# Attention block on one Trainium2 core: transposing U by DMA and normalising it on GpSimd, with a dense q tile moved into the prologue

## Chip, cores, metric

One core of one Trainium2 chip. The metric is the device time of one execution in microseconds (us), median of several; the fast executions of one kernel within a set of runs spread by 0.1 to 0.6% here.

## Reference

A layer norm, multi-query attention (32 query heads of 20, one shared key and value head), and a dense feed-forward branch, all added to the input:

```python
B, S, D, H = 1, 2048, 640, 32          # head size 20
F = 1728
xn = layernorm(x)
q = (xn @ wq) as [B, H, S, 20];  k = xn @ wk;  v = xn @ wv
p = softmax(einsum("bhqd,bkd->bhqk", q, k) * 20 ** -0.5)
o = einsum("bhqk,bkd->bhqd", p, v) as [B, S, 640] @ wo
out = x + o + silu(xn @ w1) @ w2       # bf16 inputs
```

The softmax needs 32 x 2048 x 2048 exponentials, and those are the bulk of the work outside TensorE.

## The kernel before

The kernel is written as a small list scheduler. It knows estimated durations, decides for each engine the order of its instructions, and then emits them. The order is fixed when the kernel is built; the chip only waits on semaphores.

A *unit* is one head and one chunk of 512 queries (128 units). Three units make a *group* (43 groups, the last has two), and a group goes through 16 key tiles, one *step* each (688 steps). A step is three score matmuls (L735) into three PSUM banks, one ACT exponential over two or three of them (L753), and, where `want_dve` allows, VectorE's approximate exponential of the third block (L767, followed by the integer additions L825 on up to three blocks at once). The results are multiplied with V and accumulated in bank 6 (L813). What stands there at a group's end is *U*: the unnormalised outputs of its three units, with the sums by which they are to be divided.

```python
def want_dve(self, t):                       # may VectorE take the third block of step t?
    if t < DVE_FROM or t % KT >= KT - NOD:
        return False
    back = sc.t["dve"] - sc.t["pe"]          # how far VectorE is behind, by the builder's estimates
    for op in sc.pend["dve"]:
        back += op.dur
    back += len(self.zblocks) * 0.6
    return back < DVE_TH

def end_group(self, g):                      # U is in bank 6: three units and their sums
    def evac(v):
        return v.tensor_copy(self.U[0:rows, up, :], self.bk(UBANK, 0, QW, 0, rows))
    sc.new("dve", ..., evac, [("UB",)], [("U", up)], ...)
    def ut(pe):                              # transpose on TensorE, back into the same bank
        for qt in range(4):
            ins = pe.matmul(self.bk(UBANK, qt * 64, qt * 64 + 64),
                            self.U[0:rows, up, qt * P:(qt + 1) * P], self.stk[0:rows, :], ...)
    ...
    sc.new("dve", 0.14, lambda v: v.reciprocal(rl, xv[:, :, :, DH]), [("UB",)], ...)
    ...                                      # DVE: o = U transposed * reciprocal, out of the same bank
```

Beside attention, TensorE computes the q tiles of later chunks, the feed-forward branch (h: L991, its product: L1053) and the output product (L1058). `PRO` lists the projection jobs of the prologue in order (v: value tiles, t: transposes, k: key tiles, q: q tiles); the first *dense* q tile, whose rows are brought into place by seven small SBUF-to-SBUF DMA copies, was queued behind the prologue (`jobs.append(qs.pop(0))`).

The softmax here doesn't subtract the row's maximum and nothing guards it: scores larger than these inputs give would overflow.

## Time and profile before

| | before |
|---|---|
| time, median of fast runs | 772.9 us |
| span in the profile | 770.8 us |
| PE / DVE / ACT / POOL busy | 737.9 / 690.1 / 724.5 / 23.5 us |
| last exponential ends | 749.8 us |
| from there to the end | 21.0 us |

In the views PE is TensorE, PEld its weight loads, DVE VectorE, ACT ScalarE, POOL GpSimd, and SPq the queue of SyncE, which issues the DMAs. A *hole* is an idle gap of ACT, the *tail* the time from the last exponential to the end.

How to read the table: three engines are 90% busy or more, so the shares do not name the bound. What tells is who waits for whom. The prediction shows these lines. In the timelines: start us, length us, engine, line, operation, count, in brackets the idle time before it.

### The profile page before, as it was taken

How to read it: one execution, taken by the hardware profiler on the slowest of the kernel's cores; microseconds unless marked ns; L12 is line 12 of the kernel's file. 1: busy time of each engine (PE TensorE's matmuls, PEld its weight loads, DVE VectorE, ACT ScalarE, POOL GpSimd, SP SyncE). 2: the span in 40 equal slices, each digit the busy share in tenths (PEclk: the TensorE clock that was granted, in tenths of full speed). 3: DMA queues.
4: the chain of work that ended last, by engine and by line, in shares of the span. 5: the costliest groups of instructions: out<-in, count | busy, mean ns of one | idle time of the engine just before them, and what ended most of it. 6: DMA issues, size and time to landing. Idle time of an engine off the chain costs nothing. (4 is left out here: it accounts for less than half of the span.)

```text
span 770.8 us, 17543 instructions
## 1 busy us (share of the span) xinstructions
PE 737.9 (96%) x6892; PEld 241.6 (31%) x6892; DVE 690.1 (90%) x1375; ACT 724.5 (94%) x780; POOL 23.5 (3%) x68
## 2 busy tenths in 40 slices
PE   8798999999999999999999999999999999999997
PEld 4332232222233333222223333332223333222334
DVE  7976999989998998999999998899998799899985
ACT  7887999999999999999999999999999999999960
POOL 5420000000000000000000000000000000000000
PEclk9988999999999999999999999999999999999999
DMA  6650000000110000000002000000020000000100
GB/s 182 163 188 8 8 14 8 9 8 15 36 35 26 18 9 25 26 9 1 1 4 50 9 25 25 19 13 3 1 36 19 18 19 18 1 2 1 29 1 35
DMA packets 33110, 21.53 MB, mean 28 GB/s; under 512 B 20838, under 2 KB 32390, under 8 KB 33030
## 3 DMA queue, kind: packets, MB, share of 16 engines
q1 hardware_dynamic: 31718, 20.36, 9.7%
q8 instruction: 56, 0.92, 0.5%
q10 hardware_dynamic: 1312, 0.05, 0.1%
q14 instruction: 24, 0.20, 0.1%
HBM read 11.36 MB, written 2.62 MB: 18 GB/s over the span
## 5 line engine op out<-in xcount | busy, mean ns | idle before, releaser
L753 ACT ACTIVATE sbt<-psall 128x1024 bf16<-128x1024 f32 (+2 forms) x688 | 692.4, 1146 | 20.5 <-PE psall L735 18.5
L767 DVE TENSOR_SCALAR sbt<-psall 128x512 int16<-128x512 f32 x572 | 383.8, 685 | 49.7 <-PE psall L735 41.0
L735 PE MATMUL psall<-sbt 32*128 32x512 bf16 x2048 | 270.7, 387 | 18.7 <-ACT sbt L753 8.9
L813 PE MATMUL psall<-sbt 128*32 128x512 bf16 x3355 | 262.8, 387 | 0.2
L825 DVE TENSOR_SCALAR sbt<-sbt 128x1536 int16<-128x1536 int16 (+2 forms) x430 | 207.7, 505 | 4.4 <-PE psall L813 2.0
L735 PEld LDWEIGHTS psall<-sbt 32*128 32x128 bf16 x2048 | 69.4, 91 | 257.7 <-ACT sbt L753 117.9
L813 PEld LDWEIGHTS psall<-sbt 128*32 128x32 bf16 x3355 | 70.7, 95 | 114.2 <-issue 68.1
L991 PE MATMUL psall<-sbt 128*128 128x512 bf16 (+1 forms) x280 | 88.9, 390 | 2.1 <-DVE sbt L1004 1.6
L1053 PE MATMUL psall<-sbt 128*128 128x320 bf16 x448 | 87.3, 303 | 1.0 <-DVE sbt L966 0.9
L1053 PEld LDWEIGHTS psall<-sbt 128*128 128x128 bf16 x448 | 35.1, 97 | 44.5 <-issue 33.2
L1004 DVE SCALAR_TENSOR_TENSOR sbt<-sbt,psall 128x512 bf16<-128x512 bf16 (+1 forms) x56 | 38.2, 682 | 3.9 <-ACT sbt L999 3.3
L999 ACT ACTIVATE sbt<-psall 128x512 bf16<-128x512 f32 (+1 forms) x56 | 39.3, 702 | 0.0
L887 DVE CAST sbt<-psall 128x512 bf16<-128x512 f32 x43 | 29.5, 685 | 4.9 <-PE psall L813 4.8
L991 PEld LDWEIGHTS psall<-sbt 128*128 128x128 bf16 (+1 forms) x280 | 19.4, 98 | 42.7 <-issue 31.1
L1058 PE MATMUL psall<-sbt 128*128 128x320 bf16 x160 | 30.4, 302 | 0.7 <-DVE sbt L1036 0.7
L959 PE MATMUL psall<-sbt 128*128 128x512 bf16 (+1 forms) x95 | 28.6, 385 | 0.0
L672 PE MATMUL psall<-sbt 128*128 128x512 bf16 (+3 forms) x91 | 25.3, 406 | 1.7 <-POOL sbt L1201 1.4
L659 PE MATMUL psall<-sbt 128*32 128x512 bf16 (+9 forms) x74 | 21.5, 346 | 0.0
L1076 DVE SCALAR_TENSOR_TENSOR sbt<-psall,sbt 128x320 bf16<-128x320 f32 x32 | 15.0, 484 | 4.1 <-PE psall L1058 3.1
L922 DVE TENSOR_TENSOR sbt<-psall,sbt 128x240 bf16<-128x240 f32 (+2 forms) x46 | 17.2, 379 | 0.2
L1058 PEld LDWEIGHTS psall<-sbt 128*128 128x128 bf16 x160 | 12.6, 97 | 13.1 <-issue 7.0
L966 DVE TENSOR_SCALAR sbt<-psall 128x512 bf16<-128x512 f32 (+1 forms) x19 | 12.9, 679 | 0.0
(79 smaller groups left out, 165.9 us busy)
## 6 DMA issues: line engine op xcount, KB each, us to landing
sbt<-in_A_x_dram SPq DMA_DIRECT2D x32, 160.0 KB, 3.0
out_dram<-sbt SPq DMA_DIRECT2D x16, 160.0 KB, 1.8
sbt<-in_B_w_dram SPq DMA_DIRECT2D x5, 432.0 KB, 5.2
sbt<-sbt SPq DMA_DIRECT2D x105, 20.0 KB
sbt<-in_B_w_dram SPq DMA_DIRECT2D x13, 160.0 KB, 5.1
sbt<-in_A_wo_dram SPq DMA_DIRECT2D x5, 160.0 KB, 6.2
sbt<-in_A_wq_dram SPq DMA_DIRECT2D x5, 140.0 KB, 3.5
sbt<-sbt SPq DMA_TRANSPOSE x25, 2.6
```

Source lines behind the costliest of these rows:

```text
L735: ins = pe.matmul(self.bk(par3 + j), self.kT[r:r + SLOT, kk, kt * P:(kt + 1) * P], self.qT[r:r + SLOT, h // 4, (x // H) % 2, :], start=Tru ...
L753: return a.activation(self.E[:, b0 * QW:(b0 + na) * QW], self.ps[:, par3 * BANK:(par3 + na) * BANK], AF.Exp, scale=ACT_SCALE)
L767: return v.tensor_scalar(self.Z[:, zs, zp * QW:(zp + 1) * QW], self.bk(bb), 0.0, ZMAX, ALU.max, ALU.min)
L813: return pe.matmul(self.bk(UBANK, 0, QW, q * SLOT, (q + 1) * SLOT), self.v[:, w, kt, :], x, start=start, stop=stop, tile_position=(0, q * ...
L825: sc.new("dve", t_dve_4x(w), lambda v, k=k: v.tensor_scalar(self.Y[:, zs, k, 0:n * QW], Z, float(PH[k + 1][0]), None, ALU.add), zk, [("Y", ...
L887: return v.tensor_copy(self.U[0:rows, up, :], self.bk(UBANK, 0, QW, 0, rows))
L959: return pe.matmul(self.bk(b, 0, QW, 0, rows), self.wq[:, k, lo:hi], self.xnT[:, k, c * QW:(c + 1) * QW], start=(k == 0), stop=(k == DC - 1))
L991: return pe.matmul(self.bk(b, 0, QW, 0, rows), self.w1[:, k, fk * P:fk * P + rows], self.xnT[:, k, c * QW:(c + 1) * QW], start=(k == 0), s ...
L999: sc.new("act", t_act(QW), lambda a: a.activation(t, src, AF.Tanh, scale=0.5), [("B", b)], [("tb", tp)], prio=X_PRIO, name=f"th{c}_{fk}")
L1004: sc.new("dve", t_dve_ps(QW), lambda v: v.scalar_tensor_tensor(out=self.hT[0:rows, fk, :], in0=t, scalar=1.0, in1=src, op0=ALU.add, op1=AL ...
L1053: return pe.matmul(self.bk(b, 0, 320), self.hT[0:rows, fk, i * P:(i + 1) * P], self.w2[0:rows, fk, e0:e0 + 320], start=(m == 0), stop=(m = ...
L1058: return pe.matmul(self.bk(b, 0, 320), self.oT[:, k, i * P:(i + 1) * P], self.wo[:, k, e0:e0 + 320], start=(m == 0), stop=(m == tot - 1))
```

## The change

The intent: bank 6 is blocked at each group's end by transpose, reciprocal and multiplication; free it as soon as it is evacuated, by transposing U from SBUF to SBUF with a DMA and normalising on GpSimd, which was idle in the loop. VectorE gets time for more exponential blocks. The first dense q tile moves ahead of the last value tiles so that its copies are early, and the scaling of the output weights is put behind the key tiles. The builder's constants are tuned again.

```diff
-NBLK = 34
+NBLK = 31                       # exponential blocks held in SBUF (room for UT and W)
-DVE_TH = 2.6
+DVE_TH = 3.0
-X_PRIO = 0.95
+X_PRIO = 1.6
-OVER = 0.2
+OVER = 0.1
-DVE_FROM = 6
-PRO = "v0 t8 t9 k2 t10 k3 k4 k5 q1 v1 k6 k7 v2 v3"
+DVE_FROM = 10
+PRO = "v0 t8 t9 k2 t10 k3 k4 k5 q1 v1 k6 k7 d0 v2 v3"
@@ the SP queue: other transfers may pass a waiting load @@
-                    lst = lst[:1]
+                    first = [o for o in lst if o.name in ("dma", "xTd")]
+                    lst = first[:1] + [o for o in lst if o.name not in ("dma", "xTd")] if first else lst
@@ new @@
+    def norm_dma(self, g, rows):
+        op = sc.dma("sp", lambda q: q.dma_start_transpose(self.UT[:, up, :, 0:rows], self.U[0:rows, up, :]), ...)
+        # GpSimd: copy 2 units, add the two partial sums of the third, add two corrections
+        pl = [(0.35, lambda v: v.tensor_copy(w[:, :, 0:2, :], ut[:, :, 0:2, 0:DH + 1])), (0.3, two)]
+        for lo, hi, i in ((0, 11, 0), (11, DH + 1, 1)):
+            pl.append((0.22, lambda v, ...: v.tensor_tensor(w[:, :, 2, lo:hi], ..., ALU.add)))
+        ...
+        sc.new("dve", 0.22, lambda v: v.reciprocal(rl, w[:, :, :, DH]), [("W", 0), ("W", 1)], ...)
+        ...                     # GpSimd: o = w * reciprocal
+            sc.new("pool", ..., lambda v, ...: v.tensor_tensor(dst, src, rb, ALU.mult), ...).lock = True
@@ end_group @@
+        if g < self.NG - 1:      # all groups but the last
+            self.pv_last.rl = sc.pend["dve"][-1]
+            self.norm_dma(g, rows)
+            return
@@ the queue behind the prologue @@
-            jobs.append(qs.pop(0))
+            qs.pop(0)
@@ weights: the five GpSimd multiplications of wo move behind the k tiles @@
```

(`lock`: the builder keeps GpSimd's instructions and VectorE's L825 apart in its estimates.)

The same lines have other numbers after the change: exponentials L753 -> L765, VectorE's blocks L767 -> L779, scores L735 -> L747, accumulation L813 -> L826, additions L825 -> L838, evacuation L887 -> L937, reciprocal L906 -> L914, feed-forward product L1053 -> L1111, output product L1058 -> L1116, q copies L974 -> L1031. New: the DMA transpose L896, GpSimd's L904, L907, L909 and L923.

More of the change, by code (lines that the diff above doesn't have):

```diff
@@ L64 @@
 DT_ISSUE = 1.28
+UT_ISSUE = 1.05
 DT = (4, 5, 6, 7, 11, 12, 13, 14, 15)
 NORM_P = 0.05
-DVE_FROM = 6
-PRO = "v0 t8 t9 k2 t10 k3 k4 k5 q1 v1 k6 k7 v2 v3"
+DVE_FROM = 10
+PRO = "v0 t8 t9 k2 t10 k3 k4 k5 q1 v1 k6 k7 d0 v2 v3"
 ACT_STATS = (2, 4, 6, 8, 9, 12)
@@ L76 @@
     __slots__ = ("eng", "dur", "fn", "deps", "prio", "seq", "end", "avail", "idx", "inc", "inc_no", "sem",
-                 "on_sched", "name", "dma", "mode", "start", "mm", "work", "kt", "na", "rs", "re", "rl", "then", "after")
+                 "on_sched", "name", "dma", "mode", "start", "mm", "work", "kt", "na", "rs", "re", "rl", "then", "after", "lock")
     def __init__(self, eng, dur, fn, deps, prio=0.0, name="", on_sched=None, mode=None):
@@ L98, in __init__ @@
         self.then = None
+        self.lock = False
 LAT = {"pe": 0.215, "act": 0.175, "dve": 0.14, "pool": 0.15, "sp": 0.0}
@@ L118, in __init__ @@
         self.held = {}
+        self.lock_end = {"dve": 0.0, "pool": 0.0}
         self.busy = defaultdict(float)
@@ L175, in ready @@
                 r = a
+        if op.lock:
+            r = max(r, self.lock_end["pool" if op.eng == "dve" else "dve"])
         return r
@@ L182, in commit @@
         if op.dma:
-            if op.name in ("oTd", "xTd"):
+            if op.name in ("oTd", "xTd", "uTd"):
                 self.dma_t = op.end
             self.dma_t = max(getattr(self, "dma_t", 0.0), op.end) + op.mode / 230e3
-            op.avail = op.end + 1.6 if op.name in ("oTd", "xTd") else max(op.end + 2.0, self.dma_t + 1.6)
+            op.avail = op.end + 1.6 if op.name in ("oTd", "xTd", "uTd") else max(op.end + 2.0, self.dma_t + 1.6)
         else:
@@ L192, in commit @@
         self.busy[e] += op.dur
+        if op.lock:
+            self.lock_end[e] = op.end
         self.held[e] = op.then
@@ L372, in alloc @@
         self.stk = sb([P, 64], BF16)
+        self.UT = sb([P, 2, 4, P], BF16)
+        self.W = sb([P, 4, 3, DH + 1], F32)
         self.hT = sb([P, FC, QW], BF16)
@@ L613, in step @@
                 self.u_last = op.after
+            if op.kt == KT - 1 and getattr(op, "rl", None) is not None:
+                self.u_last = [op.rl]
             if not self.pv_started:
@@ L795, in do_S @@
         pv.kt = kt
+        self.pv_last = pv
         pv.na = na
@@ L826, in flush_z @@
                 self.Y[:, zs, k, 0:n * QW], Z, float(PH[k + 1][0]), None, ALU.add), zk,
-                [("Y", zs, k, i) for i in range(n)], prio=4.0 + 0.1 * k, name=f"y{k}")
+                [("Y", zs, k, i) for i in range(n)], prio=4.0 + 0.1 * k, name=f"y{k}").lock = True
         ts = []
@@ L877, in flush_z @@
         self.zblocks = []
+    def norm_dma(self, g, rows):
+        sc = self.sc
+        us = self.groups[g]
+        up = g % 2
+        op = sc.dma("sp", lambda q: q.dma_start_transpose(self.UT[:, up, :, 0:rows], self.U[0:rows, up, :]),
+                    [("U", up)], [("UT", up)], rows * QW * 2, sem=self.s_UT[up], name="uTd")
+        op.dur = UT_ISSUE
+        self.ut_cnt[up] += 1
+        op.inc_no = self.ut_cnt[up]
+        ut = self.UT[:, up, :, :].rearrange("p q (i j) -> p q i j", j=SLOT)
+        w = self.W
+        if rows == P:
+            two = lambda v: v.tensor_tensor(w[:, :, 2, :], ut[:, :, 2, 0:DH + 1], ut[:, :, 3, 0:DH + 1], ALU.add)
+        else:
+            two = lambda v: v.tensor_copy(w[:, :, 2, :], ut[:, :, 2, 0:DH + 1])
+        pl = [(0.35, lambda v: v.tensor_copy(w[:, :, 0:2, :], ut[:, :, 0:2, 0:DH + 1])), (0.3, two)]
+        for lo, hi, i in ((0, 11, 0), (11, DH + 1, 1)):
+            pl.append((0.22, lambda v, lo=lo, hi=hi, i=i: v.tensor_tensor(
+                w[:, :, 2, lo:hi], w[:, :, 2, lo:hi], ut[:, :, i, DH + 1:DH + 1 + hi - lo], ALU.add)))
+        for n, (d, fn) in enumerate(pl):
+            sc.new("pool", d, fn, [("UT", up)], [("W", n if n < 2 else 1)], prio=0.5, name=f"w{g}").lock = True
+        rl = self.rL[:, up, :, :]
+        sc.new("dve", 0.22, lambda v: v.reciprocal(rl, w[:, :, :, DH]), [("W", 0), ("W", 1)], [("rL", up)], prio=U_PRIO,
+               name=f"rcp{g}")
+        for c in sorted(set(x // H for x in us)):
+            js = [j for j, x in enumerate(us) if x // H == c]
+            h0, m = us[js[0]] % H, len(js)
+            dst = self.o[:, c % 2, :, h0 * DH:(h0 + m) * DH].rearrange("p q (i d) -> p q i d", d=DH)
+            src = w[:, :, js[0]:js[0] + m, 0:DH]
+            r0 = rl[:, :, js[0]:js[0] + m]
+            rb = bass.AP(self.rL, r0.offset, [list(r0.ap[0]), list(r0.ap[1]), [1, m], [0, DH]])
+            sc.new("pool", 0.15 + 4 * m * DH * 0.00186, lambda v, dst=dst, src=src, rb=rb: v.tensor_tensor(
+                dst, src, rb, ALU.mult), [("W", 0), ("W", 1), ("rL", up)], [("o", c % 2, h0 + i) for i in range(m)],
+                prio=0.5, name=f"nrm{g}").lock = True
+            self.norm_made[c] += m
+            self.try_oT(c)
     def end_group(self, g):
@@ L888, in end_group @@
         sc.new("dve", t_dve_ps(QW), evac, [("UB",)], [("U", up)], prio=U_PRIO, name=f"Uev{g}")
+        sc.pend["dve"][-1].name = f"Uev{g}"
+        if g < self.NG - 1:
+            self.pv_last.rl = sc.pend["dve"][-1]
+            self.norm_dma(g, rows)
+            return
         def ut(pe):
@@ L970, in consume @@
             ops = []
-            for h in range(lo // DH, -(-hi // DH)):
+            heads = range(lo // DH, -(-hi // DH))
+            for h in heads:
                 a, z = max(lo, h * DH), min(hi, h * DH + DH)
@@ L975, in consume @@
                     self.qT[r:r + z - a, h // 4, c % 2, :], self.qd[a - lo:z - lo, sl, :]), [("qd", sl)],
-                    [("q", c, h, lo), ("qb", c % 2, h)], (z - a) * QW * 2, sem=sem, name="qdma"))
+                    [("qb", c % 2, h)], (z - a) * QW * 2, sem=sem, name="qdma"))
                 ops[-1].dur = 0.74
+            sc.note(ops[-1], (), [("q", c, h, lo) for h in heads])
             for op in ops:
@@ L1152, in prologue @@
         self.out_cnt = [0] * 3
+        self.s_UT = [sem(f"UT{i}") for i in range(2)]
+        self.ut_cnt = [0, 0]
         self.s_oT = [sem(f"oT{i}") for i in range(4)]
@@ L1355, in prologue @@
                            for c in range(DC)], ("wo",), P * D * 2)
-        for c in range(DC):
-            pool(0.7, lambda g, c=c: g.tensor_scalar(self.wo[:, c, :], self.wo[:, c, :], 2.0, 1.0, ALU.mult, ALU.mult),
-                 [("wo",)], [("wo",)])
         for par in range(2):
@@ L1404, in consume @@
                        [("kT1", j)], prio=1.0, name=f"k1_{j}")
+                if j == KT // 2 - 1:
+                    for c in range(DC):
+                        pool(0.7, lambda g, c=c: g.tensor_scalar(self.wo[:, c, :], self.wo[:, c, :], 2.0, 1.0, ALU.mult,
+                                                                 ALU.mult), [("wo",)], [("wo",)], prio=2.0)
             return Job(f"kv{j}", mms, [("xnT", 2 * j), ("xnT", 2 * j + 1), ("wk",)], consume)
@@ L1436, in prologue @@
             self.misc.append(tr_job(n) if w[0] == "t" else k_job(n) if w[0] == "k" else self.q_job(n)
-                             if w[0] == "q" else v_job(4 * n, 4 * n + 4))
+                             if w[0] == "q" else self.qd_job(0, n) if w[0] == "d" else v_job(4 * n, 4 * n + 4))
 def bass_kernel(nc, *args):
```

## The prediction

> **What bounds the kernel now.** I read the page's busy shares first. PE, ACT and DVE all stand at 90% or more, so the shares alone do not name the bound.
>
> ```profile
> PE 737.9 (96%) x6892; PEld 241.6 (31%) x6892; DVE 690.1 (90%) x1375; ACT 724.5 (94%) x780; POOL 23.5 (3%) x68
> ```
>
> Next the busy table by stage (columns: stretch, its length, then busy us and instructions of PE, PEld, DVE, ACT, POOL, then granted clock, DMA share, GB/s), cut at the prologue, the start of the attention loop, its body and the end.
>
> ```profile
> 17.00:50.00 33.00, 26.87 (x232) 10.34 (x229) 27.61 (x83) 27.85 (x30) 15.12 (x34) 0.90 0.67 205
> 50.00:75.00 25.00, 20.86 (x196) 6.21 (x193) 16.86 (x36) 19.75 (x20) 0.00 (x0) 0.86 0.03 7
> ...
> 140.00:230.00 90.00, 86.73 (x827) 25.69 (x828) 84.92 (x163) 90.00 (x95) 0.00 (x0) 1.00 0.09 22
> 230.00:320.00 90.00, 89.12 (x886) 30.07 (x878) 80.23 (x155) 88.72 (x89) 0.00 (x0) 1.00 0.07 20
> ...
> 725.00:750.00 25.00, 24.66 (x213) 9.13 (x214) 22.09 (x49) 18.72 (x25) 0.00 (x0) 1.00 0.07 15
> ```
>
> From 75 to 725 us (eight such stretches, 650 us) ACT is busy 645.3 us, so idle only 4.7. ACT loses time only at the edges: 5.2 us in 17 to 50, 5.2 in 50 to 75, 6.3 in 725 to 750; after 750 it has nothing left and the last 21 us are TensorE, DVE and the stores. PE looks as full, but the waits table shows its weight loads standing for ACT's exponentials, and ACT hardly ever for PE:
>
> ```profile
> PEld psall L735 <- ACT sbt L753: 117.9, 305, 1.2
> DVE sbt L767 <- PE psall L735: 41.0, 91, 3.5
> ...
> ACT sbt L753 <- PE psall L735: 18.5, 33, 3.3
> ```
>
> So ACT's exponentials (L753) set the pace; DVE (L767 takes over one 512-column block of a step's exponentials where the builder finds DVE not too far behind) has slack. The groups by form give the exchange rate:
>
> ```profile
> L753 ACT ACTIVATE sbt<-psall 128x1024 bf16<-128x1024 f32 x562 | 544.8, 1087 | 13.3 <-PE psall L735 11.6 <-PE psall L813 1.3
> L767 DVE TENSOR_SCALAR sbt<-psall 128x512 int16<-128x512 f32 x572 | 383.8, 685 | 49.7 <-PE psall L735 41.0 <-PE psall L813 6.5
> ...
> L753 ACT ACTIVATE sbt<-psall 128x1536 bf16<-128x1536 f32 x113 | 169.5, 1502 | 2.4 <-PE psall L735 2.2
> ```
>
> A step with its third block on DVE costs ACT 1502 - 1087 = 415 ns less. The rest of ACT is fixed work. **A gain must therefore come from blocks moved off ACT, or from ACT's holes at the edges.**
>
> Last the timeline of one group's end, and of the one big hole at the start:
>
> ```profile
> 305.23 0.68 DVE L887 CAST sbt<-psall 128x512 bf16<-128x512 f32 x1
> ...
> 306.03 0.28 PE L893 MATMUL psall<-sbt 128*128 128x64 bf16 x4
> ...
> 306.90 0.22 DVE L906 RECIPROCAL sbt<-psall 128x12 f32<-128x12 f32 x1
> ...
> 307.58 0.39 DVE L922 TENSOR_TENSOR sbt<-psall,sbt 128x240 bf16<-128x240 f32 x1
> ...
> 308.39 0.83 PE L813 MATMUL psall<-sbt 128*32 128x512 bf16 x12
> ```
>
> ```profile
> 58.40 5.34 SPq L974 DMA_DIRECT2D sbt<-sbt  x7
> ...
> 65.02 0.14 PEld L735 LDWEIGHTS psall<-sbt 32*128 32x128 bf16 x3 [3.29 <-issue]
> 65.05 0.61 PE L735 MATMUL psall<-sbt 32*128 32x512 bf16 x3 [2.82 <-DMA sbt<-sbt]
> ```
>
> Bank 6, which collects P times V, is held from the evacuation at 305.23 to the normalising multiply that ends at 307.97; only then may the next group accumulate. And the first dense q tile's seven small copies are issued at 58.40, but wanted soon after 62: scores wait until 65.05.
>
> **What the Trainium skill says.** (1) "PSUM — Partial Sum Buffer", The four PSUM rules: GpSimd cannot touch PSUM. That is why the change brings U through SBUF and a DMA. In the trace before, GpSimd indeed has no instruction on psall. (2) "SBUF — State Buffer", Who interferes with whom: a GpSimd instruction and a VectorE one in a 2-port mode exclude each other for a whole instruction. The 430 L825 additions are such candidates (bf16-sized, SBUF to SBUF, 549 ns for 1536 columns). Before, GpSimd is idle after the prologue, so nothing shows it in the loop; in the prologue the same 128x256 GpSimd form takes 0.51 us at 32.03 and 0.87 at 36.92, which fits but does not prove it. (3) "GPSIMD Engine Reference", 3.1 Elementwise: about 2.6 cycles an element with two inputs, at 1.2 GHz. The trace has only 4-element two-input ones, 0.20 us each at 0.28 us spacing. (4) "DMA: Bandwidth & Descriptors", Anatomy of one DMA: some 2 us fixed for a DMA. The trace agrees for transposes: 2.6 us from issue to landing (median of 25), SP taken about 1.2.
>
> **The change part by part.** The counts come from the order of the built programs, before against after.
>
> *Normalising.* For 42 of 43 groups the PE transpose goes (168 of L893), bank 6 is free once evacuated, some 2 us sooner by the timeline above, and DVE loses 44 multiplies: 40 of 397 ns, less about 85 ns by which neighbours overlap (two L767 in a row take 1.28, so 0.60 apart at 685 long), is 40 x 0.31 = 12.5, with four smaller ones 13.2 us. The 42 reciprocals stay, from SBUF.
>
> *What DVE gets.* The builder turns that, with the higher limit DVE_TH, into 598 L767 blocks instead of 572: 26 x 0.60 = +15.6 us. The L825 additions go from 324/66/40 (1536/1024/512 columns) to 336/90/8: 12 x 0.47 + 24 x 0.34 - 32 x 0.20 = +7.4. Net DVE -13.2 + 15.6 + 7.4 = +10 us on 690: about 700 of 757, 92%. Still not the bound, with less room.
>
> *What ACT loses.* 26 steps go from 1536 to 1024 columns: 26 x 0.415 = **-10.8 us**, on the path one for one, since ACT is idle under 1% of the loop. DVE_FROM 10 puts four early blocks back on ACT where it has holes anyway, so the loop itself loses a little more: I count **-1**.
>
> *PE.* 42 x 0.28 = 11.8 us of transposes go; 58 more accumulation matmuls, four side by side in about 0.22, add 3. Room where PE is fullest (230 to 320, the output products; ACT idle 1.3 there, 1.2 and 2.2 in its two sister stretches): **-2**.
>
> *Dense q tile in the prologue.* It is the same work, moved. Its copies then follow the weight loads on SP, which end about 45.6 (L1186 from 37.87 for 7.69): 45.6 + 5.3 + 2 = 53, before the need at 62. ACT idled 2.68 at 65.71, then 0.93 and 0.48, the granted clock falling to 0.73 in 60 to 70. I count **-4**.
>
> *Output weights.* Five GpSimd multiplications stand behind the last k tiles in both programs; **0**.
>
> *GpSimd.* Five instructions a group, 168 to 240 elements at the most: est. 0.40 + 0.40 + 0.35 + 0.35 + 0.75 = 2.2 us, from the 256-column form's 0.5, the 0.28 spacing and the skill's 2.6 cycles. 42 groups make some 95 us, 15% of the span: far from a bound.
>
> *The new chain.* Evacuation end to reciprocal: transpose 2.6 + four GpSimd instructions 1.5 + handovers 0.1 = 4.2 us. In the new DVE order, the instructions between a group's evacuation and its reciprocal sum to 4.9 us in the median (3.5 the least), and DVE idles a tenth besides. So the in-order DVE should mostly find the sums ready. Late SP, and L825 additions blocked by GpSimd (est. one of ten a group, 0.25 us each, half of it absorbed): **+2**.
>
> Sum: -10.8 - 1 - 2 - 4 + 2 = -15.8. 772.9 - 15.8 = 757.1; I say **757.0 us**.
>
> **Rivals.** (a) *DVE blocks at the reciprocal.* For it: only 0.7 us of margin in the median, SP is in order and must also issue q copies (5.3 us a tile) and stores that wait. Against: the builder lets ready transposes pass. A stall of 0.4 us a group is 17 us of DVE; I would expect half on ACT's path: 764 to 766. (b) *The GpSimd and VectorE exclusion* costs each L825 more than I think: 430 x 25 ns on the path would eat the 10.8: 767. (c) *Nothing is gained in the loop because PE is the true bound* and ACT only looks full: then only the prologue's 4 and PE's own 2 to 5 remain: 764 to 767. Against it stands ACT's wait of 118 us imposed on PE. (d) *Better than summed*: earlier release of bank 6 also mends the end (6.3 us of ACT holes in 725 to 750) and the prologue's 5.2: 750.
>
> **Range and chances.** The 10.8 is a count times a duration and the 4 a visible hole; the stalls can cost up to 10, the edges can give 7. Eight in ten: **749 to 766**. The 2% line is at 757.5, next to my number: **faster 0.52, same 0.46, slower 0.02**.
>
> **What would show it.** Right: L753 588/87/13 times with ACT idle still under 10 us in the loop; no score wait on an SBUF-to-SBUF DMA near 62; reciprocal waits on GpSimd under 5 us in all; GpSimd busy 80 to 110 us; DVE near 700. Wrong: DVE waits on POOL above 15 us, mean L825 up by over 30 ns, ACT idle in the body over 15 us, or SP's transposes landing later than 3.5 us.

## More of the kernel before

The exponentials stop 21 us before the end, and then TensorE finishes its feed-forward and output products:

```profile
748.80 1.03 ACT L753 ACTIVATE sbt<-psall 128x1024 bf16<-128x1024 f32 x1 [0.37 <-PE psall L735]
...
753.62 5.44 PE L1053 MATMUL psall<-sbt 128*128 128x320 bf16 x35
```

## The result, and the profile after

| | before | after |
|---|---|---|
| time, median of 4 fast runs | 772.9 us | **761.15 us** (760.63 to 761.35) |
| ratio of fast runs | | 0.985 (95%: 0.983 to 0.987) |
| span in the profile | 770.8 us | 759.5 us |
| last exponential ends | 749.8 us | 731.8 us |
| from there to the end | 21.0 us | 27.7 us |

Ratios here and below are the mean time of one kernel's fast runs over that of the other's of the same rounds, so not quite the ratio of the medians quoted. Executions over 1.5% slower than the fastest of the same kernel are left out of the means. Differences between experiments are taken from their ratios times 772.9, because the kernel before had medians of 772.8, 773.7 and 772.1 us in the three sets of experiments.

So the kernel got 1.5% faster, 4 us short of the 757.0 predicted and inside the range, but short of the 2% to which the prediction gave 0.52. First the busy shares after:

```profile
PE 724.4 (95%) x6758; PEld 235.0 (31%) x6816; DVE 699.8 (92%) x1361; ACT 712.6 (94%) x780; POOL 107.5 (14%) x280
```

ACT lost 11.9 us of work, DVE gained 9.7, GpSimd 84.0. (About 35 of the 280 feed-forward h matmuls have no record in this trace; PE's count is not to be compared closely.) The busy table by stage, with the columns of the prediction's table:

```profile
17.00:50.00 33.00, 27.04 (x259) 11.82 (x260) 25.69 (x81) 25.20 (x27) 14.44 (x34) 0.95 0.67 208
50.00:75.00 25.00, 23.05 (x196) 6.67 (x197) 22.30 (x41) 24.57 (x28) 3.13 (x9) 1.00 0.09 19
...
230.00:320.00 90.00, 89.29 (x880) 28.71 (x881) 87.26 (x162) 89.78 (x94) 11.66 (x30) 1.00 0.10 26
...
712.00:739.00 27.00, 26.84 (x212) 10.51 (x210) 21.60 (x49) 15.88 (x23) 2.97 (x6) 1.00 0.13 26
739.00:760.00 21.00, 14.79 (x103) 9.28 (x101) 10.10 (x22) 0.00 (x0) 0.00 (x0) 0.91 0.08 31
```

ACT's idle time in 50 to 75 fell from 5.25 to 0.43 us, but in 17 to 50 it rose from 5.15 to 7.8. From 75 to 712 it is 3.2 us. The waits after (engine and line that waits, what for, us in total, times, longest):

```profile
POOL sbt L907 <- DMA sbt<-sbt: 547.8, 42, 20.1
PEld psall L747 <- ACT sbt L765: 108.7, 275, 1.3
...
DVE sbt L779 <- PE psall L747: 22.1, 63, 2.1
...
DVE sbt L914 <- POOL sbt L909: 2.8, 5, 0.8
```

GpSimd's 547.8 us are its idle time until the next group and cost nothing. What matters is the last line: the in-order VectorE stands for GpSimd five times only. The groups by form:

```profile
L765 ACT ACTIVATE sbt<-psall 128x1024 bf16<-128x1024 f32 x588 | 565.1, 1088 | 10.5 <-PE psall L826 6.5 <-PE psall L747 3.3
L779 DVE TENSOR_SCALAR sbt<-psall 128x512 int16<-128x512 f32 x598 | 401.1, 684 | 27.4 <-PE psall L747 22.1 <-PE psall L826 0.8
L838 DVE TENSOR_SCALAR sbt<-sbt 128x1536 int16<-128x1536 int16 x336 | 184.8, 561 | 2.1
L765 ACT ACTIVATE sbt<-psall 128x1536 bf16<-128x1536 f32 x87 | 130.0, 1505 | 0.6 <-PE psall L747 0.5
L923 POOL TENSOR_TENSOR sbt<-sbt 128x240 bf16<-128x240 f32 x40 | 25.9, 647 | 39.8 <-DVE sbt L914 39.4 <-ACT sbt L765 0.4
```

And one group's end in the timeline:

```profile
265.80 0.68 DVE L937 CAST sbt<-psall 128x512 bf16<-128x512 f32 x1
266.55 1.20 SPq L896 DMA_TRANSPOSE sbt<-sbt  x1
266.91 0.61 PE L826 MATMUL psall<-sbt 128*32 128x512 bf16 x8
...
269.08 0.33 POOL L907 CAST sbt<-sbt 128x168 f32<-128x168 bf16 x1 [11.06 <-DMA sbt<-sbt]
...
271.39 0.22 DVE L914 RECIPROCAL sbt<-sbt 128x12 f32<-128x12 f32 x1
```

The evacuation ends at 266.48 and the next group accumulates from 266.91, 0.43 us later; in the prediction's timeline of before it was 305.91 to 308.39, 2.48 us. Over 42 groups, read from the two traces, the median of this gap fell from 2.20 to 0.72 us, so by 1.5 us; the pair shown is a good one. The new chain behind it takes 4.9 us to the reciprocal and holds nobody in this group.

Last, the hole at the start and the end of the exponentials, from the timelines of ACT and PE:

```profile
43.19 8.78 ACT L765 ACTIVATE sbt<-psall 128x1024 bf16<-128x1024 f32 x9 [6.50 <-PE psall L826]
...
730.09 1.67 ACT L765 ACTIVATE sbt<-psall 128x512 bf16<-128x512 f32 x2 [2.15 <-PE psall L747]
...
736.07 11.77 PE L1111 MATMUL psall<-sbt 128*128 128x320 bf16 x77
```

**The ledger.** Up to its last exponential ACT has its busy time and its idle time, nothing else. Busy: 724.5 to 712.6, -11.9 us. Idle: 749.8 - 724.5 = 25.3 to 731.8 - 712.6 = 19.2, -6.1 us. Together the last exponential comes 18 us earlier, more than predicted for the whole kernel. But the tail behind it grew by 6.7 us: TensorE still has a run of 77 feed-forward product matmuls of 11.77 us where before it was 35 of 5.44, which is 6.3 of the 6.7. So two questions are for experiments: why is there a 6.50 us hole in the prologue that was not there, and why does the end give 6.7 us back?

### The profile page after: what moved, and what is told of

The parts are those of the page before. It is cut to its first block, busy times and chain, and to the rows that moved or that the text cites. A ratio compares the mean times of both kernels' runs of the same rounds, so it can differ in the third digit from the quotient of the medians.

```text
span 759.5 us, 17804 instructions
## 1 busy us (share of the span) xinstructions
PE 724.4 (95%) x6758; PEld 235.0 (31%) x6816; DVE 699.8 (92%) x1361; ACT 712.6 (94%) x780; POOL 107.5 (14%) x280
## 5 line engine op out<-in xcount | busy, mean ns | idle before, releaser
L765 ACT ACTIVATE sbt<-psall 128x1024 bf16<-128x1024 f32 (+1 forms) x688 | 679.7, 1131 | 14.5 <-PE psall L747 7.0
L779 DVE TENSOR_SCALAR sbt<-psall 128x512 int16<-128x512 f32 x598 | 401.1, 684 | 27.4 <-PE psall L747 22.1
L747 PE MATMUL psall<-sbt 32*128 32x512 bf16 x2048 | 269.1, 384 | 12.9 <-ACT sbt L765 6.3
L826 PE MATMUL psall<-sbt 128*32 128x512 bf16 x3413 | 265.6, 384 | 2.7 <-DVE sbt L937 1.3
L838 DVE TENSOR_SCALAR sbt<-sbt 128x1536 int16<-128x1536 int16 (+2 forms) x434 | 218.8, 527 | 2.2
L747 PEld LDWEIGHTS psall<-sbt 32*128 32x128 bf16 x2048 | 69.6, 91 | 264.6 <-ACT sbt L765 108.7
L826 PEld LDWEIGHTS psall<-sbt 128*32 128x32 bf16 x3413 | 67.0, 94 | 113.9 <-issue 73.2
L907 POOL CAST sbt<-sbt 128x168 f32<-128x168 bf16 x42 | 15.3, 364 | 547.8 <-DMA sbt<-sbt 547.8
L1111 PE MATMUL psall<-sbt 128*128 128x320 bf16 x448 | 82.5, 302 | 0.0
L1049 PE MATMUL psall<-sbt 128*128 128x512 bf16 (+1 forms) x245 | 74.9, 384 | 4.9 <-issue 3.1
L1111 PEld LDWEIGHTS psall<-sbt 128*128 128x128 bf16 x448 | 36.1, 97 | 40.2 <-issue 27.8
L923 POOL TENSOR_TENSOR sbt<-sbt 128x240 bf16<-128x240 f32 (+2 forms) x44 | 27.7, 631 | 41.9 <-DVE sbt L914 41.5
L1116 PE MATMUL psall<-sbt 128*128 128x320 bf16 x160 | 30.9, 303 | 0.7 <-DVE sbt L1094 0.7
L937 DVE CAST sbt<-psall 128x512 bf16<-128x512 f32 x43 | 29.4, 683 | 1.8 <-PE psall L826 1.8
L671 PE MATMUL psall<-sbt 128*32 128x512 bf16 (+7 forms) x98 | 29.2, 363 | 0.0
L909 POOL TENSOR_TENSOR sbt<-sbt 128x44 f32<-128x44 f32 x84 | 27.8, 331 | 6.6
L1015 PE MATMUL psall<-sbt 128*128 128x512 bf16 (+1 forms) x80 | 25.2, 394 | 2.2 <-issue 2.2
L1128 DVE SCALAR_TENSOR_TENSOR sbt<-psall,sbt 128x320 f32<-128x320 f32 x16 | 7.9, 492 | 10.2 <-PE psall L1111 9.7
```

The lines of the kernel that those rows point to most:

```text
L671: return pe.matmul(self.bk(UBANK, 0, n, 0, 32), self.zero[:, 0:32], self.zero[:, 0:n], start=False, stop=False, tile_position=(0, 0), skip ...
L747: ins = pe.matmul(self.bk(par3 + j), self.kT[r:r + SLOT, kk, kt * P:(kt + 1) * P], self.qT[r:r + SLOT, h // 4, (x // H) % 2, :], start=Tru ...
L765: return a.activation(self.E[:, b0 * QW:(b0 + na) * QW], self.ps[:, par3 * BANK:(par3 + na) * BANK], AF.Exp, scale=ACT_SCALE)
L779: return v.tensor_scalar(self.Z[:, zs, zp * QW:(zp + 1) * QW], self.bk(bb), 0.0, ZMAX, ALU.max, ALU.min)
L826: return pe.matmul(self.bk(UBANK, 0, QW, q * SLOT, (q + 1) * SLOT), self.v[:, w, kt, :], x, start=start, stop=stop, tile_position=(0, q * ...
L838: sc.new("dve", t_dve_4x(w), lambda v, k=k: v.tensor_scalar(self.Y[:, zs, k, 0:n * QW], Z, float(PH[k + 1][0]), None, ALU.add), zk, [("Y", ...
```

## The experiments

All are correct. "After" stands for the changed kernel; edits are against it unless said otherwise.

| label | median us (range of fast runs) | ratio to before (95%) | last exponential ends | tail |
|---|---|---|---|---|
| after | 761.15 (760.63 to 761.35) | 0.985 (0.983 to 0.987) | 731.8 | 27.7 |
| pe_norm | 771.21 (769.57 to 774.10) | 0.998 (0.996 to 1.001) | 741.4 | 30.9 |
| d0_alone | 769.34 (768.19 to 770.44) | 0.995 (0.994 to 0.997) | 746.2 | 21.0 |
| cap_mid | 770.54 (769.42 to 772.60) | 0.997 (0.995 to 0.999) | 739.4 | 27.7 |
| cap_late | 763.21 (762.23 to 764.83) | 0.988 (0.986 to 0.990) | 743.4 | 17.0 |
| no_d0 | 758.67 (757.48 to 759.04) | 0.981 (0.979 to 0.983) | 729.1 | 27.8 |
| v_first | 758.22 (757.44 to 759.13) | 0.981 (0.979 to 0.983) | 729.1 | 27.8 |
| from6 | 761.42 (761.11 to 763.87) | 0.987 (0.984 to 0.989) | 731.9 | 27.8 |
| v_from6 | 764.51 (764.09 to 765.97) | 0.990 (0.988 to 0.992) | 734.5 | 27.8 |
| chain4 | 771.54 (769.23 to 771.98) | 0.997 (0.995 to 0.999) | (slow profile) | |
| chain4b | 769.97 (one run) | | 740.4 | 27.8 |
| nrm3 | 761.59 (761.04 to 762.33) | 0.985 (0.983 to 0.987) | 731.5 | 27.8 |
| v_cap40 | 757.08 (755.85 to 757.27) | 0.980 (0.978 to 0.981) | 730.0 | 25.3 |

The last two columns come from the one profiled run of each.

### Which part of the change brings it: pe_norm and d0_alone

`pe_norm` keeps everything but the new normalisation:

```diff
-        if g < self.NG - 1:
+        if False:
```

> The changed kernel with its main part undone: every group's U is transposed by TensorE into bank 6 and normalised there by DVE, as before; the builder's other new values, the prologue and the 31 blocks stay. The builder gives DVE 585 blocks instead of 598, so ACT has 13 x 0.415 = 5.4 us more, and bank 6 is held some 2 us longer a group. Theory (the gain is the normalisation's move off DVE and off bank 6): 772 to 778 us, no better than before, since the new values were tuned to the new path. Rival (the gain comes from the builder's values and not from the move): 765 us or less.

Measured: ratio 0.998 against 0.985, so **the normalisation is worth 10 us** among these constants, and the rest of the change hardly 2 (0.998 is not clear of 1). The builder finds room for 585 VectorE blocks here, against 598 in after and 572 before. That is 13 blocks, at 0.415 us 5.4 us of ACT; the other half of the 10 us is not the blocks. The traces show where most of the 10 us is lost (count the exponentials in ACT's order; the last chunk starts with step 512). When step 511's exponential ends, the profiled run of `pe_norm` is 3.9 us behind after; its last chunk then takes 216.5 us against 207.6. There TensorE has 44 more transpose matmuls and 10 more h matmuls to do than in after, at a granted clock of 0.983 against 0.992 (this run is the slowest of its four). How much the sooner free bank saves is not shown.

`d0_alone` is the kernel before with the dense tile in the prologue and nothing else:

```diff
-PRO = "v0 t8 t9 k2 t10 k3 k4 k5 q1 v1 k6 k7 v2 v3"
+PRO = "v0 t8 t9 k2 t10 k3 k4 k5 q1 v1 k6 k7 d0 v2 v3"
-            jobs.append(qs.pop(0))
+            qs.pop(0)
```

> The kernel before with the dense q tile moved into the prologue in front of the last two v jobs, nothing else. Theory of the prediction: the 2.8 us wait for SBUF-to-SBUF copies near 65 us goes, and the time falls by 3 to 4 us (ratio 0.995 to 0.996). Rival, from the runs without the tile: it delays the v jobs and the first accumulation, with 34 blocks and narrow steps from the seventh on the hole is smaller than in the changed kernel, and the two cancel: within 1.5 us of before (0.998 to 1.002).

Measured: 3.6 us by the ratio. The prediction's 4 us for this part is right *for the kernel before*. Taken with `pe_norm`, which contains the same move and gains only 1.5 us, it suggests that the other edits (constants, SP queue, weights), without the new normalisation, cost about 2 us; the two intervals overlap, so this is not shown.

### Who sets the pace, and where: cap_mid and cap_late

Both take about the same number of VectorE blocks away and so put them on ACT, `cap_mid` in groups 11 to 21 (the middle of the program), `cap_late` from group 32 on (the last chunk):

```diff
-        if t < DVE_FROM or t % KT >= KT - NOD:
+        if t < DVE_FROM or t % KT >= KT - NOD or (t // KT in range(11, 22) and t % KT in (3, 7, 11)):
```

```diff
-        if t < DVE_FROM or t % KT >= KT - NOD:
+        if t < DVE_FROM or t % KT >= KT - NOD or (t // KT >= 32 and t % KT in (3, 7, 11)):
```

> The changed kernel with 33 steps of the second chunk (groups 11 to 21, steps 3, 7 and 11 of 16) refused to DVE; the builder then gives DVE about 577 blocks instead of 598, so ACT has about 21 x 0.415 = 8.7 us more to do in the second chunk. Theory 1 (ACT bounds the loop everywhere): 761 + 8 to 9 = 769 to 770 us, ratio about 0.995. Rival (TensorE bounds, ACT only looks full): 761 to 763 us, or faster, as every block on DVE costs TensorE more matmuls.

> The same refusal of 33 steps, but in the last chunk (groups 32 on); about 574 blocks on DVE, 24 x 0.415 = 10 us more for ACT there. If ACT bounds the last chunk too (theory 1): about 770 us, as in the second chunk. If TensorE bounds the last chunk, because it still has both output products and the tail after the last exponential to do (the changed kernel has 27.7 us after its last exponential, the one before 21.0): the added ACT work is hidden, the time is 760 to 763 us, and the stretch after the last exponential shrinks by 7 us or more.

Measured: `cap_mid` has 577 blocks and is 9.6 us slower than after by the ratios, 0.46 us for each of its 21 blocks (7.6 us or 0.36 by the spans of the profiled runs); ACT has 0.415 more to do for each. Each edit also lets the builder order everything anew; but the loss lies where the blocks were taken: the exponentials of steps 176 to 351 take 187.0 us instead of 176.7. Its blocks and wide exponentials, by form:

```profile
L779 DVE TENSOR_SCALAR sbt<-psall 128x512 int16<-128x512 f32 x577 | 388.2, 683 | 40.1 <-PE psall L747 34.9 <-PE psall L826 0.4
...
L765 ACT ACTIVATE sbt<-psall 128x1536 bf16<-128x1536 f32 x108 | 161.7, 1505 | 0.6 <-PE psall L747 0.5
```

`cap_late` has 574 blocks, 24 fewer, and is only 2.2 us slower, 0.09 us a block (its interval overlaps that of after). Its timeline at the end shows where it went:

```profile
742.38 1.02 ACT L765 ACTIVATE sbt<-psall 128x1024 bf16<-128x1024 f32 x1 [2.42 <-PE psall L747]
...
745.39 3.33 PE L1111 MATMUL psall<-sbt 128*128 128x320 bf16 x21
```

The last exponential is 11.6 us later than in after, and the tail shrinks from 27.7 to 17.0: while ACT is slower, TensorE does its feed-forward products beside it instead of behind it. **So in the middle of the program ACT is the bound, and in the last chunk TensorE is.** In after's trace PE is busy 19.6 of the last 19.8 us before the last exponential ends (712.0 to 731.8), and ACT 15.9. From the end of step 511's exponential to the end of the program after takes 207.6 us and `cap_late` 208.2, with 24 blocks more for ACT. TensorE has more to do there than in the other chunks: half of the 448 feed-forward product matmuls, since the last chunk's own cannot be put off to a later one.

How many of the 26 blocks gained lie there? Counting the exponentials of three blocks in ACT's order in the two built programs: -4 in steps 0 to 9 (DVE_FROM), +5 in 10 to 47, +5 in 48 to 175, +7 in 176 to 351, +6 in 352 to 511, +7 in 512 to 671, 0 behind. So seven lie where a block is worth 0.09 and not 0.415 us.

### The hole in the prologue: no_d0, v_first, from6, v_from6

The first accumulation (L826) stands behind the value tiles, since it needs them. In after the dense tile stands ahead of these, the steps up to the tenth are three blocks wide, and there are 31 blocks of SBUF for exponentials instead of 34. Ten steps of three are 30 blocks: ACT then has nowhere to write until the first accumulation has read, hence the hole. Its 6.50 us are at the upper end: five other experiments with the same order of exponentials there (`pe_norm`, `cap_mid`, `cap_late`, `chain4b`, `nrm3`) show 4.8 to 4.9. Four kernels vary the order. `no_d0` puts the tile back behind the prologue:

```diff
-PRO = "v0 t8 t9 k2 t10 k3 k4 k5 q1 v1 k6 k7 d0 v2 v3"
+PRO = "v0 t8 t9 k2 t10 k3 k4 k5 q1 v1 k6 k7 v2 v3"
-            qs.pop(0)
+            jobs.append(qs.pop(0))
```

> The changed kernel with the dense q tile taken back out of the prologue (its job queued after the prologue as before); everything else as changed. Theory of the prediction: the tile's early copies were worth 4 us (no wait for an SBUF-to-SBUF copy near 62 us), so this run is 3 to 4 us slower than the changed kernel: about 765 us, ratio to before near 0.990, and the score wait near 62 us of about 3 us is back. Rival, from the changed trace: the tile stands in front of the last two v jobs, so accumulation starts later, and ACT finds the 31 exponential blocks full (hole of 6.50 us before 43.19); then taking it out shortens that hole by 2 us or more and brings the copy wait back, so the time stays within 1.5 us of 761.

`v_first` leaves it in the prologue but last:

```diff
-PRO = "v0 t8 t9 k2 t10 k3 k4 k5 q1 v1 k6 k7 d0 v2 v3"
+PRO = "v0 t8 t9 k2 t10 k3 k4 k5 q1 v1 k6 k7 v2 v3 d0"
```

> The changed kernel with the dense q tile still in the prologue but behind the last two v jobs instead of in front of them. If the 6.50 us hole of ACT before 43.19 us comes from accumulation starting late (v tiles late, all 31 exponential blocks full), the hole shrinks to 4.5 us or less, no copy wait comes near 62 us, and the time falls by 1.5 to 3 us to 758 to 759.5 (ratio about 0.982). If the hole is set by something else (bank 6, the weights still loading), it keeps its length and the time is 761 within 1 us.

Measured: both at 0.981, 2.7 to 3 us faster than after; the intervals just touch that of after, and the profiled spans say the same (756.9 twice, against 759.5). The ACT timeline of `v_first` shows the hole:

```profile
40.19 6.95 ACT L765 ACTIVATE sbt<-psall 128x1024 bf16<-128x1024 f32 x7 [2.85 <-PE psall L826]
```

It is 2.85 us, 2 less than the usual 4.8. In `v_first` and `no_d0` ACT is busy 52.8 and 53.1 us of 17 to 75, in after and the five kernels with its order 49.8 to 51.6 (mean 50.8): again 2 of the 3 us. And `no_d0` did *not* bring the wait for the copies near 62 us back, though it undoes the move: its dense tile runs at 43.8 us and its copies start at 48.5 anyway. So **within the changed kernel, moving the dense tile ahead of the value tiles cost about 3 us and brought nothing**. Which of the other edits (X_PRIO, the SP queue) makes the tile early by itself I did not separate.

`from6` and `v_from6` give VectorE its blocks from step 6 again, in after and in `v_first`:

```diff
-DVE_FROM = 10
+DVE_FROM = 6
```

> The changed kernel with DVE_FROM 6 in place of 10 and nothing else: 599 VectorE blocks against 598; the dense q tile keeps its place ahead of the last value tiles in the list, but the builder now puts the first accumulation before the dense tile's matmuls. If the 6.50 us hole came from the two together (wide steps and the dense tile ahead of the first accumulation), it shrinks under 3 us and the time is 758 to 759.5, with the last exponential 2 to 3.5 us earlier than 731.8. If the dense tile's place alone made it, it stays over 5 us and the time within 1 us of 761.2.

> The dense q tile behind the value tiles, as in v_first, and the VectorE blocks allowed from step 6 again, as before the change: 602 VectorE blocks against 598 there, and the first accumulation stands two score groups earlier in TensorE's order. Theory (what v_first still loses in the prologue is ACT's last 2.85 us hole before the first accumulation, made by the late start of the VectorE blocks): the hole shrinks under 1.5 us and the time is 756 to 757.5 against 758.2 of v_first. Rival (the start's holes are given back by TensorE at the end, where 27.9 us stand after the last exponential): within 0.6 us of v_first, with the tail longer by what the last exponential gained.

Measured: in `from6` the hole shrinks to 2.31 us, as the theory of the two causes together says, and yet the time is no better (0.987 against 0.985, overlapping intervals): waits for scores of 1.12, 2.17 and 0.88 us come behind it, and ACT's busy time in 17 to 75 is 49.4 us, no more than in after. Filling one hole moved it. `v_from6` was a miss for both my theories: 7 us *slower* than `v_first`. Its PE timeline:

```profile
67.73 0.61 PE L747 MATMUL psall<-sbt 32*128 32x512 bf16 x6 [0.50 <-DMA sbt<-sbt]
```

and its SP timeline:

```profile
60.41 5.34 SPq L1031 DMA_DIRECT2D sbt<-sbt  x7
```

With the early blocks allowed, the builder puts the first accumulation and the value tiles ahead of the dense tile, whose copies are then issued at 60.41 instead of 45.66 us in `v_first`: the wait that this part of the change was made to remove is back, with an ACT hole of 2.36 us before it. ACT's busy time in 17 to 75 is 47.5 us against 52.8, 5.2 of the 7 us. DVE_FROM 10, which I had booked as a loss of blocks, is in truth what keeps the dense tile early when it stands last.

### Has the new chain margin: chain4, chain4b

Three more GpSimd copies into unused SBUF ahead of the reciprocal, some 1.0 us of GpSimd a group. The order on PE, DVE, ACT and SP is that of after (line numbers are one higher):

```diff
-        pl = [(0.35, lambda v: v.tensor_copy(w[:, :, 0:2, :], ut[:, :, 0:2, 0:DH + 1])), (0.3, two)]
+        pl = [(0.35, lambda v: [v.tensor_copy(self.X[:, x] if x < 3 else w[:, :, 0:2, :],
+                                              ut[:, :, 0:2, 0:DH + 1]) for x in range(4)][-1]), (0.3, two)]
```

> The changed kernel, same order on every engine, with three more copies of U's transpose (into unused space) in front of the four GpSimd instructions that the reciprocal waits for: the chain from evacuation to reciprocal grows by about 3 x 0.33 = 1.0 us in each of 42 groups. The changed kernel waited at the reciprocal 2.8 us in all, 5 times. Theory (a margin of some 0.7 us that now covers it): DVE's wait on GpSimd grows to 10 to 30 us and the time by 4 to 10 us. Rival (the margin is far larger, or DVE's waits are not on the path): under 1.5 us more.

> The same kernel as chain4 again, for a profile in the fast state: three more GpSimd copies ahead of the reciprocal in each group's chain, some 1.0 us a group. Time again 769 to 772. If the late reciprocal stands in VectorE's way (rival a), its wait on GpSimd rises from 2.8 us to 15 to 35 us in all, and ACT's idle time in the body rises by 5 us or more. If it is instead the exclusion between GpSimd and VectorE, the wait stays under 8 us and the 1536-column additions rise from 561 to over 600 ns.

Measured: `chain4` 0.997, 9.5 us slower than after. Its profiled run fell in the slow state (851.97 us at a granted clock of 0.752), so it was profiled again as `chain4b`, a single run at 769.97 us with clock 0.998. From its waits, and its groups by form:

```profile
DVE sbt L915 <- POOL sbt L910: 18.9, 28, 1.8
```

```profile
L839 DVE TENSOR_SCALAR sbt<-sbt 128x1536 int16<-128x1536 int16 x336 | 185.3, 562 | 2.1
L908 POOL CAST sbt<-sbt 128x168 f32<-128x168 bf16 x168 | 56.8, 380 | 539.8 <-DMA sbt<-sbt 539.8
```

VectorE's wait for GpSimd rose from 2.8 to 18.9 us, 28 groups of 42 instead of 5; ACT's idle time from 75 to 712 rose from 3.2 to 9.3 us and its last exponential came 8.6 us later. The additions stayed at 562 ns, so it is not the two engines excluding each other. **Rival (a) is real, and the kernel has missed it by less than the 1.0 us a group that were added.**

### Does GpSimd slow VectorE's additions: nrm3

The normalising multiplication three times (twice into unused space), behind the reciprocal, where nothing waits for it soon:

```diff
-            sc.new("pool", ..., lambda v, ...: v.tensor_tensor(dst, src, rb, ALU.mult), ...)
+            sc.new("pool", ..., lambda v, ...: [v.tensor_tensor(
+                self.X[:, x, :, j0:j0 + m, :] if x < 2 else dst, src, rb, ALU.mult) for x in range(3)][-1], ...)
```

> The changed kernel, same order on every engine, with the normalising multiply done three times on GpSimd (twice into unused space): 42 x 2 x 0.6 = 50 us more of GpSimd, all behind the reciprocal, so only its meetings with DVE's 2-port additions and a later o can cost. In the changed kernel 28 of 336 wide additions began while GpSimd ran and took 0.66 us instead of 0.55. Theory (exclusion is real but small): their mean rises by another 10 to 20 ns, 4 to 7 us of DVE in all, and the time by 0 to 3 us. Rival (exclusion is what ate the gain): 5 us or more slower.

Measured: 0.985, as after. Its groups by form:

```profile
L839 DVE TENSOR_SCALAR sbt<-sbt 128x1536 int16<-128x1536 int16 x336 | 190.8, 579 | 2.1
...
L924 POOL TENSOR_TENSOR sbt<-sbt 128x240 bf16<-128x240 f32 x120 | 77.1, 670 | 43.0 <-DVE sbt L915 41.9 <-ACT sbt L766 1.0
```

51 us more GpSimd work lengthens the additions from 561 to 579 ns, 6 us of VectorE in all, and the time does not move: VectorE has that much slack. Rival (b) has an effect that can be seen and no price here.

### A better version: v_cap40

`v_first`, and no VectorE block in steps 4 and 10 of the last three groups, where a block moved to ACT is nearly free:

```diff
-PRO = "v0 t8 t9 k2 t10 k3 k4 k5 q1 v1 k6 k7 d0 v2 v3"
+PRO = "v0 t8 t9 k2 t10 k3 k4 k5 q1 v1 k6 k7 v2 v3 d0"
-        if t < DVE_FROM or t % KT >= KT - NOD:
+        if t < DVE_FROM or t % KT >= KT - NOD or (t // KT >= 40 and t % KT in (4, 10)):
```

> v_first, with the VectorE block refused in two steps of each group from group 40 on (595 blocks against 598), so that VectorE and TensorE work the last groups with less beside them. If TensorE alone ends the program, giving blocks back to ACT there is free and the time within 0.7 us of v_first's 758.2, the tail after the last exponential shorter by 1 to 3 us. If VectorE's backlog holds the end, it is 1 us or more faster. If ACT still counts there, up to 1.2 us slower (3 blocks by 0.415).

Measured: 757.08 us, ratio 0.980 (0.978 to 0.981). The last exponential comes 1 us later than in `v_first` and the tail is 2.6 us shorter. Against `v_first` that is 1.0 us by the ratios, from different sets of runs with overlapping intervals, so not shown to be better; against before and after it is the fastest kernel here, 2.0% and 0.5%.

## Why the prediction was right or wrong

- **ACT's -10.8 us for 26 blocks.** The counts are right to the instruction (588, 87 and 13 exponentials), and ACT is busy 11.9 us less. The step that failed is the words "on the path one for one". They hold in the middle (`cap_mid`: 0.46 us a block) and not in the last chunk (`cap_late`: 0.09), where seven of the 26 lie. The reason given, ACT idle under 1% of the loop, was no proof: another engine can be just as full beside it, and set the pace.
- **The sum was one for the last exponential, not for the end.** This is the step that cost most. It said -15.8 us, and the last exponential came 18.1 us earlier. I took the 21 us behind it as fixed, with no term for them. They became 27.7. The two differences, -2.3 and +6.7, are the 4.4 us by which the profiled span (-11.3) missed the sum. That two misses of opposite sign left the total only 4 us off is partly luck.
- **Where the tail's 6.7 us come from.** Counted from the end of step 511's exponential, before is 13.3 us behind after, so the whole gain and more was made by then. In the last chunk ACT reaches its last exponential in 179.9 us instead of 184.7: its holes fell by 3.2 us and its work by 1.6 (seven blocks less, three feed-forward activations more). TensorE followed neither: the last chunk as a whole takes 207.6 us instead of 205.6, and 206.9 to 208.2 in the eight experiments other than `pe_norm`, `d0_alone` and the lengthened chain. So 4.8 of the 6.7 are ACT's lead, and 2.0 are lost. TensorE's weight loads there say what it does more: 44 transpose matmuls fewer, 28 accumulation matmuls more, and 90 h matmuls instead of 78, because the builder left more of them for the end; twelve cost some 2.6 us (an estimate from their spacing of 0.215 us). With 0.28 us for four transpose matmuls and 0.22 for four accumulations, as the prediction has them, these sum to +1.0 of the 2.0 us; the rest stays open. The new normalisation is not needed for a longer tail: `pe_norm` keeps the old one with the new constants, has 100 h matmuls there and the longest tail of all. From its PE timeline:

```profile
744.60 16.00 PE L1111 MATMUL psall<-sbt 128*128 128x320 bf16 x105
```

`d0_alone`, with the old constants, has the old tail of 21.0 us. Which of the new constants puts the work off, no run separates.
- **Dense q tile, -4.** The copies come in time and the wait near 62 us is gone; alone on the kernel before the move is worth 3.6 us (`d0_alone`); and ACT's idle time in 17 to 75 did fall, from 10.4 to 8.2 us (6.4 to 8.2 over all kernels with this order). Still the step "It is the same work, moved" failed: in the changed kernel the tile would have been early without the move (`no_d0`), and its place delays the first accumulation. Left out or put last, it is 3 us faster.
- **DVE_FROM, -1.** Not shown: `from6` has no price or gain within the intervals, and `v_from6` 7 us in the other direction, by way of TensorE's order.
- **PE, -2, and the sooner free bank.** The next accumulation starts 2.05 us sooner after the evacuation in the lines shown, 1.5 in the median. `pe_norm` says that the normalisation is worth 10 us, of which its 13 blocks can explain 5.4 at most; I had booked only 2 for the rest, and most of it lies in the last chunk, where TensorE sets the pace. That more was gained is seen in the ledger: ACT's idle time outside 17 to 75 fell by 3.9 us.
- **The chain, 4.2 us, and stalls, +2.** Over 42 groups, read from the trace, the time from the end of the evacuation to the start of the reciprocal has a minimum of 4.22 and a median of 5.0 us, as VectorE often comes later itself; the transposes take 2.55 us from SP's start to GpSimd's. VectorE waits 2.8 us for GpSimd. Right, and the margin as thin as said (`chain4b`).
- **GpSimd** was predicted at 95 us for the 42 groups; the page has 107.5 with some 23 from the prologue, 86 by the groups. Right that it is no bound. (Its "only 4-element" ones overlooked three two-input instructions of 10 to 21 elements in the prologue, 0.21 to 0.27 us; nothing rested on it.)
- **Output weights, 0.** The five multiplications have the same place in GpSimd's order in both built programs, so no run was spent on it.
- **Rivals.** (a) did not happen but is less than 1 us a group away; (b) has no effect on the time; (c) was half right: TensorE is the bound in the last chunk and not in the middle, and the first chunk was not tested; (d), a mended end, went the other way: ACT's holes at the end shrank, and the tail grew by more.

What stays open: which edit brings the dense tile early in `no_d0`, which constant leaves TensorE more for the last chunk, and how the 10 us of `pe_norm` divide between the free bank, the missing transposes and the order which the builder then finds. The profiled run of `pe_norm` was its slowest (774.10 us), so its last two columns are good to some 3 us only.

## What to carry to other kernels

Price a gain stage by stage: take the same number of blocks from the pacing engine in the middle and at the end, and see what each costs, before a busy share is read as a bound. When work is moved ahead, look at what it moves back: the first release of a full buffer can matter more than the wait that is removed. And where an engine runs in order, a new chain to it is free only up to its slack; adding a known delay measures that slack in one run.

## What the Trainium skill lacked or had wrong

- "VectorE: DVE Perf Modes", The three transpose paths, gives the DMA transpose only for 128x128 (1309 ns). Here one of 128x512 bf16 (four such squares), SBUF to SBUF, keeps SP 1.20 us and takes 2.55 us (median of 42) from SP's start to the first instruction that waits for it: not four times as much.
- "GPSIMD Engine Reference", 3.1 Elementwise, gives a rate and, for small instructions, no fixed part as a number. Here the normalising multiplication (f32 in, bf16 out) took 385 ns for 80 elements a partition, 553 for 160 and 647 for 240 (means of 2, 2 and 40). That is 1.64 ns an element from 80 to 240, 2.0 cycles at the page's 1.2 GHz where it has 2.6, and a fixed part of some 0.25 us (an estimate from the same line). The case is not quite the page's: the second input repeats each value 20 times, the three points do not lie on one line (2.1 and 1.2 ns an element), and spans on GpSimd are rough.
- "SBUF — State Buffer", Who interferes with whom, has the exclusion but no price for a pair like this one. Of 336 wide additions in the trace after, the 28 that began while GpSimd was at work took 658 ns in the mean and the others 553; tripling one GpSimd instruction raised the mean of all from 561 to 579 ns and left the time where it was.
